# Batch 0's value block means as TensorE products with a banded matrix, instead of a second load and a tree of adds

## The chip, the cores and the metric

One core of one Trainium2 chip runs the whole program as a single launch. The metric is device time in microseconds (us). Engines: PE is TensorE (PEld its weight loads), DVE is VectorE, ACT is ScalarE, POOL is GpSimd, SP is SyncE, which here issues every DMA.

## What is computed

Block-sparse attention followed by two feed-forward networks, all in float32. Cut to what matters here:

```python
batch, n_heads, seq, head_dim = 2, 8, 768, 64
block, window, nb = 32, 16, 24                    # nb = seq // block
k_sum = k.reshape(B, H, nb, block, D).max(axis=3)
v_sum = v.reshape(B, H, nb, block, D).mean(axis=3)     # the value block means
scores_l = scale * q @ k.T        # kept only where |i - j| < window
scores_s = scale * q @ k_sum.T + log(block)
a = softmax(concat([masked scores_l, scores_s]))
attn = a @ concat([v, v_sum])
x = attn as (1536 tokens, 512)
x = prelu(x @ w_in, alpha) @ w_out              # 512 -> 2048 -> 512
out = silu(x @ w2_in) @ w2_out                  # 512 -> 2048 -> 512
```

## The kernel before

Heads are handled in pairs: 128 partitions hold 2 heads of 64 dimensions. There are 2 batches, 4 pairs, and blocks of 256 queries, so an attention step is (block, pair), and `order` lists 24 of them: batch 0's first two blocks pair by pair, then the rest block by block. A step n runs through `scores` (PE makes `sc` in a PSUM tile that has one buffer, DVE scales and masks it into `t` and takes its maximum `nm`), `exps` (ACT, `e` and the sums `sm`), `normalize` (DVE's reciprocal `rs`, then POOL multiplies `e`), `turn` (PE transposes `e` into `pt`, ACT copies it to `pT`) and `values` (PE multiplies `pT` with the value tile `vs` into `o`, ACT and DVE split that into `xh` and `xl` for the networks). Below, sc(n), t(n) and so on are those of step n.

A value tile `vs` has 120 rows for each of 12 sub-blocks of 64 queries: 96 rows are the window's raw values, 24 rows are the block means of the whole sequence. In an even sub-block the means are rows 0 to 23 and the window rows 24 to 119, in an odd one the window is rows 0 to 95 and the means are rows 96 to 119. The window rows come by two DMAs per pair (`vs<-in_vw`). For the means, `load_v` loads the same values a second time, transposed (`in_vT`, 384 KB per pair); `prep_v1` adds them down with two POOL adds (L482, 128x384 and 128x192) and one DVE reduction (`vr`, L485); `prep_v2` transposes `vr` on PE (L491) into the PSUM tile `pv`, and four ACT instructions (L495) scale it by 1/32 and copy it into the 12 places of `vs`. For batch 0 the transposed values lie in the half of the later output buffer `y` that `y_v` names; for batch 1 they go through the pool `stage`, whose 2 buffers they share with raw weights.

The weights come as raw 512 KB pieces (`load_next`, L116). A raw piece W(n) is converted (`conv_next`) by three DVE instructions (L142, L146, L149), one ACT cast (`wh`) and one POOL subtraction (`wl`). The first three raw pieces lie in the other half of `y` (`y_w`), the others in `stage`; a `stage` buffer is free again when DVE has read it.

The order of the first 100 us is a list of operations with hand-set due times (`AT_KEYS` and so on); a scheduling pass then orders each engine's instructions. Engines run their own list in order. SP issues the DMAs in one list, so a DMA that must wait for a buffer holds those behind it. `first_in` (L281 to L283, `ps<-xh,wl` and so on) is the first network product; the rest of the program after the attention is feed-forward products on PE.

Of the kernel before, what the change touches and what calls it, by code (L numbers as in the profile page):

```python
# [18 lines left out]
SUB = 64  # L19
PAD = WINDOW  # L20
WIN = SUB + 2 * PAD
P = 128
# [15 lines left out]
def tile_blocks_attention_mlps(  # L38
# [9 lines left out]
    consts: bass.AP,  # L48
    out: bass.AP,
# [34 lines left out]
    y_v = y.rearrange("p a n -> p (a n)")[:, :NPAIR * S].rearrange("p (a n) -> p a n", n=S)  # L84
    y_w = y.rearrange("p a n -> p (a n)")[:, NPAIR * S:].rearrange("p (a n w) -> p a n w", n=512, w=2)
# [341 lines left out]
    with ExitStack() as scope0:  # L427
# [4 lines left out]
        ps_s = scope0.enter_context(tc.tile_pool(name="ps_s", bufs=1, space=bass.MemoryType.PSUM))  # L432
        cst = kv.tile([P, P + 4 * NC], F32, name="cst", bufs=1)
        ident = cst[:, 0:P]
        mask = cst[:, P:]

# [8 lines left out]
        def load_v(b, p):  # L445
            if b == 0:
                t = y_v[:, p]
            else:
                t = stage.tile([P, 512, 2], F32, name="raw").rearrange("p n w -> p (n w)")[:, :S]
            nc.sync.dma_start(out=t, in_=vT[b, p])  # L450
            vt_t[b, p] = t
            t = kv.tile([NC, NSUB, P], F32, tag="vs", name="vs")
            vs_t[b, p] = t
            nc.sync.dma_start(out=t[NB:, 0::2], in_=vw[b, p, 0])
            nc.sync.dma_start(out=t[:WIN, 1::2], in_=vw[b, p, 1])
# [32 lines left out]
        def prep_v2(b, p):  # L488
            s_ = vs_t[b, p]
            pt = ps_mm.tile([P, 512], F32, tag="mm", name="pv")  # L490
            nc.tensor.transpose(pt[:NB, :P], vr_t.pop((b, p)), ident)  # L491

            def spread(s0, s1):
                for at in (s_[:NB, 2 * s0:2 * s1:2], s_[WIN:, 2 * s0 + 1:2 * s1:2]):
                    nc.scalar.activation(  # L495
                        out=at,
                        in_=pt[:NB, 0:P].unsqueeze(1).to_broadcast([NB, s1 - s0, P]),
                        func=AF.Copy,
                        scale=1.0 / BLOCK,
                    )  # L500
# [169 lines left out]
        for k, (blk, p) in enumerate(order[:2 * NPAIR]):  # L670
# [4 lines left out]
            if k == 0:  # L675
                at(first, lambda: nc.sync.dma_start(out=cst, in_=consts))
            if blk == 0:
                at(first, load_v, 0, p)
# [16 lines left out]
        def block_sums(b, p):  # L695
            prep_v1(b, p)
            if b:
                staged[0] -= 1
                flush()
# [102 lines left out]
def _layout(q, k, v, moe_w_in, moe_w_out, moe_alpha, moe2_w_in, moe2_w_out):  # L802
# [31 lines left out]
    for t, first in enumerate((0, P, S - P)):  # L834
# [5 lines left out]
        m[t, SUB:, :WIN] = np.where(ok, 0.0, -1000000000.0)[SUB:]  # L840
    consts = np.concatenate(
# [11 lines left out]
        "consts": np.ascontiguousarray(consts),  # L853
    }
# [19 lines left out]
```

## Time and profile before

| | us |
|---|---|
| median of 3 runs | 608.69 (608.2 to 609.58) |
| span of the profiled execution, first to last instruction | 604.6 |
| median less span: what lies around the instructions | 4.1 |
| PE busy | 576.8 (95% of the span) |
| DVE busy | 424.0 (70%) |
| ACT busy | 277.5 (46%) |
| POOL busy | 72.3 (12%) |

For the profiled execution the profile gives the span and no time of its own beside it, so the 4.1 us are taken from the median of the runs. A share of busy time is a mean over the span: the first 70 us (loads, attention, weight conversion) look quite different from the rest, in which PE runs products almost without a gap. A row of the timeline has the start, the duration, the engine, the line, output and inputs, the shape, the number of instructions merged into it, and in brackets how long the engine sat idle before and what ended that.

### The profile page before, as it was taken

The numbers are of one execution on the slowest core, as the hardware profiler recorded it, in microseconds if no ns is written. First come the engines' busy times: TensorE is split into PE (matmuls) and PEld (weight loads), VectorE is DVE, ScalarE is ACT, GpSimd is POOL, SyncE is SP. The second block draws the span as 40 slices with busy tenths as digits, with TensorE's granted clock in tenths as the row PEclk, the third lists the DMA queues.
The fourth block names the chain that finished last, engine by engine and source line by source line (L and its number), as shares of the span: only waits on it lengthen the run. The fifth ranks groups of instructions, "written<-read, shape, count | busy, mean of one in ns | idle before, by whom it ended". The sixth has DMA issues, their size and how long they took to land.

```text
span 604.6 us, 8927 instructions
## 1 busy us (share of the span) xinstructions
PE 576.8 (95%) x3428; PEld 483.5 (80%) x3428; DVE 424.0 (70%) x747; ACT 277.5 (46%) x636; POOL 72.3 (12%) x69
## 2 busy tenths in 40 slices
PE   2777999999999999999999999999999999999997
PEld 1556788999888888888888888888888888888886
DVE  3899979548995484349696879885972499965312
ACT  2768977654543341424544645543621245333200
POOL 2657654232100000000000000000000000000000
PEclk9988999999999999999999999999999999999999
DMA  9958754002351040003022002333130032200112
GB/s 263 341 193 260 231 147 140 2 2 70 140 154 56 0 140 0 1 1 112 28 69 70 1 1 79 131 117 93 32 108 0 1 111 96 73 1 0 54 69 88
DMA packets 31771, 52.54 MB, mean 87 GB/s; under 512 B 2288, under 2 KB 20976, under 8 KB 31728
## 3 DMA queue, kind: packets, MB, share of 16 engines
q1 hardware_dynamic: 31728, 51.97, 27.2%
q8 instruction: 27, 0.44, 0.3%
q14 instruction: 16, 0.13, 0.1%
HBM read 48.82 MB, written 3.15 MB: 86 GB/s over the span
## 4 chain that ended last, share of the span: by engine, by line
PE 82%; DVE 9%; DMA 3%; ACT 2%; SPq 1%; issue 1%; POOL 0%; DVEq 0%; POOLq 0%
PE ps L281 27%; PE ps L282 27%; PE ps L283 27%; DVE w L146 2%; DMA y<-in_w 1%; DVE w L149 1%; DMA vs<-in_vw 1%; DVE w L142 1%; DVE t L531 1%; DVE sm L557 1%; DVE nm L540 1%; PE o L579 1%; DVE kT L465 1%; ACT e L548 1%; DMA raw<-in_w 1%
## 5 line engine op out<-in xcount | busy, mean ns | idle before, releaser
L281 PE MATMUL ps<-xh,wl 128*128 128x512 f32 (+1 forms) x352 | 127.5, 367 | 1.2 <-ACT xh L587 1.2
L282 PE MATMUL ps<-xl,wh 128*128 128x512 f32 (+1 forms) x352 | 127.9, 364 | 0.0
L283 PE MATMUL ps<-xh,wh 128*128 128x512 f32 (+1 forms) x352 | 127.4, 363 | 0.0
L282 PE MATMUL ps<-gl,wh 128*128 128x512 f32 (+1 forms) x240 | 83.3, 348 | 0.0
L283 PE MATMUL ps<-gh,wh 128*128 128x512 f32 (+1 forms) x240 | 82.9, 346 | 0.0
L281 PE MATMUL ps<-gh,wl 128*128 128x512 f32 (+1 forms) x240 | 82.5, 350 | 0.0
L336 ACT CAST gh<-g 128x512 fp32r<-128x512 f32 x96 | 59.3, 622 | 46.2 <-PE ps L283 24.2
L281 PEld LDWEIGHTS ps<-xh,wl 128*128 128x128 f32 x352 | 66.5, 191 | 12.4 <-POOL e L560 1.4
L282 PEld LDWEIGHTS ps<-xl,wh 128*128 128x128 f32 x352 | 67.3, 191 | 10.2 <-issue 0.2
L283 PE MATMUL ps<-wh,gh 128*128 128x512 f32 (+1 forms) x196 | 75.4, 385 | 0.0
L283 PEld LDWEIGHTS ps<-xh,wh 128*128 128x128 f32 x352 | 67.3, 191 | 10.1
L282 PE MATMUL ps<-wl,gh 128*128 128x512 f32 (+1 forms) x196 | 75.4, 385 | 0.0
L281 PE MATMUL ps<-wh,gl 128*128 128x512 f32 (+1 forms) x196 | 75.2, 385 | 0.1
L337 DVE TENSOR_TENSOR gl<-g,gh 128x512 fp32r<-128x512 f32 x84 | 57.5, 687 | 20.7 <-ACT gh L336 20.3
L394 DVE TENSOR_TENSOR y<-ps,y 128x512 f32<-128x512 f32 x48 | 32.8, 689 | 45.4 <-PE ps L283 45.2
L324 ACT ACTIVATE g<-ps 128x512 f32<-128x512 f32 (+1 forms) x50 | 29.0, 579 | 70.8 <-PE ps L283 69.9
L155 ACT CAST wh<-w 128x512 fp32r<-128x512 f32 x64 | 39.3, 622 | 48.0 <-DVE w L149 43.5
L328 DVE SCALAR_TENSOR_TENSOR g<-m,nal,g 128x512 f32<-128x512 f32 (+1 forms) x60 | 41.4, 705 | 25.0 <-ACT m L325 24.9
L281 PEld LDWEIGHTS ps<-gh,wl 128*128 128x128 f32 x240 | 45.2, 189 | 6.6 <-issue 0.5
L282 PEld LDWEIGHTS ps<-gl,wh 128*128 128x128 f32 x240 | 45.4, 189 | 6.1 <-POOL gl L337 0.2
L283 PEld LDWEIGHTS ps<-gh,wh 128*128 128x128 f32 x240 | 45.3, 189 | 5.6
L146 DVE SCALAR_TENSOR_TENSOR w<-raw,w 128x512 uint32<-128x512 uint32 x61 | 44.6, 741 | 0.3
(82 smaller groups left out, 867.1 us busy)
## 6 DMA issues: line engine op xcount, KB each, us to landing
raw<-in_w SPq DMA_DIRECT2D x61, 512.0 KB, 3.8
vs<-in_vw SPq DMA_DIRECT2D x16, 288.0 KB, 5.6
kT<-in_kT SPq DMA_DIRECT2D x8, 480.0 KB, 5.2
q<-in_qT SPq DMA_DIRECT2D x24, 128.0 KB, 4.1
out<-y SPq DMA_DIRECT2D x11, 256.0 KB, 2.0
y<-in_vT SPq DMA_DIRECT2D x4, 384.0 KB, 6.5
y<-in_w SPq DMA_DIRECT2D x3, 512.0 KB, 7.7
raw<-in_vT SPq DMA_DIRECT2D x4, 384.0 KB, 4.5
```

The costliest lines, as they stand in the source:

```text
L142: nc.vector.tensor_scalar(out=w, in0=high, scalar1=3, scalar2=0x3FFFFFFF, op0=ALU.logical_shift_left, op1=ALU.bitwise_and,)
L146: nc.vector.scalar_tensor_tensor(out=w, in0=high, scalar=0xC0000000, in1=w, op0=ALU.bitwise_and, op1=ALU.bitwise_or)
L149: nc.vector.scalar_tensor_tensor(out=w, in0=low, scalar=29, in1=w, op0=ALU.logical_shift_right, op1=ALU.bitwise_or)
L155: nc.scalar.copy(out=hi, in_=w)
L281: nc.tensor.matmul(ps, all_, bh, start=first, stop=False)
L282: nc.tensor.matmul(ps, ah, bl, start=False, stop=False)
L283: nc.tensor.matmul(ps, ah, bh, start=False, stop=last)
L324: nc.scalar.activation(out=g[:, j * w:(j + 1) * w], in_=ps, func=AF.Relu)
L328: nc.vector.scalar_tensor_tensor(out=g[:, at], in0=m[:, at], scalar=nal[:, f + j:f + j + 1], in1=g[:, at], op0=ALU.mult, op1=ALU.add,)
L336: nc.scalar.copy(out=gh, in_=g)
L337: (nc.gpsimd if early else nc.vector).tensor_tensor(out=gl, in0=g, in1=gh, op=ALU.subtract)
L394: nc.vector.tensor_tensor(out=at, in0=src, in1=at, op=ALU.add)
```

## The change

Four edits, all about batch 0's value means:

- `load_v` no longer loads `in_vT` for batch 0, and `block_sums` runs `prep_v1` for batch 1 alone. Batch 1 stays as it was.
- A small constant `band` (128 x 2 x 44, 1/32 on the block each row belongs to, 0 elsewhere) is loaded once, after `cst`. `prep_v2` of batch 0 forms the 24 means in PSUM as the sum of 12 products, one per sub-block: the sub-block's 96 or 120 rows of `vs`, times the slice of `band` that picks its blocks. The copies out of PSUM scale by 1.
- Even sub-blocks are multiplied with all 120 rows, so the 24 mean rows must hold finite numbers first: POOL sets them to 0 (4 MEMSETs).
- `y_v` is gone and `y_w` covers all of `y`: six raw pieces lie in `y` instead of three.

```diff
-    y_v = y.rearrange("p a n -> p (a n)")[:, :NPAIR * S].rearrange("p (a n) -> p a n", n=S)
-    y_w = y.rearrange("p a n -> p (a n)")[:, NPAIR * S:].rearrange("p (a n w) -> p a n w", n=512, w=2)
+    y_w = y.rearrange("p a n -> p (a n)").rearrange("p (a n w) -> p a n w", n=512, w=2)
...
+        NBAND = 2 * NB - 4
+        band = kv.tile([P, 2, NBAND], F32, name="band", bufs=1)
...
         def load_v(b, p):
-            if b == 0:
-                t = y_v[:, p]
-            else:
+            if b:
                 t = stage.tile([P, 512, 2], F32, name="raw").rearrange("p n w -> p (n w)")[:, :S]
-            nc.sync.dma_start(out=t, in_=vT[b, p])
-            vt_t[b, p] = t
+                nc.sync.dma_start(out=t, in_=vT[b, p])
+                vt_t[b, p] = t
...
+            if b == 0:
+                nc.gpsimd.memset(t[:NB, 0::2], 0.0)
...
-            nc.tensor.transpose(pt[:NB, :P], vr_t.pop((b, p)), ident)
+            if b:
+                nc.tensor.transpose(pt[:NB, :P], vr_t.pop((b, p)), ident)
+            else:
+                for n in range(NSUB):
+                    rows, at = (WIN if n % 2 else NC), NB - 4 - 4 * (n // 2)
+                    nc.tensor.matmul(
+                        pt[:NB, :P], band[:rows, n % 2, at:at + NB], s_[:rows, n],
+                        start=n == 0, stop=n == NSUB - 1,
+                    )
...
-                        scale=1.0 / BLOCK,
+                        scale=1.0 / BLOCK if b else 1.0,
...
+                at(first, lambda: nc.sync.dma_start(out=band, in_=bands))
...
         def block_sums(b, p):
-            prep_v1(b, p)
             if b:
+                prep_v1(b, p)
                 staged[0] -= 1
                 flush()
```

The scheduling pass gives each engine a new order. Three places matter.

SP, the queue of loads, after the first key, query and `cst` loads (`kT` and `q` are keys and queries, `y<-in_w` and `raw<-in_w` raw weights). Before:

```order
L450 DMA y<-in_vT 128x768
L454 DMA vs<-in_vw 96x6x128
L455 DMA vs<-in_vw 96x6x128
L460 DMA q<-in_qT 128x256
L442 DMA kT<-in_kT 128x6x160
L460 DMA q<-in_qT 128x256
L450 DMA y<-in_vT 128x768
L454 DMA vs<-in_vw 96x6x128
L455 DMA vs<-in_vw 96x6x128
L460 DMA q<-in_qT 128x256
L116 DMA y<-in_w 128x1024
L442 DMA kT<-in_kT 128x6x160
```

and now:

```order
L687 DMA band<-in_bands 128x88
L456 DMA vs<-in_vw 96x6x128
L457 DMA vs<-in_vw 96x6x128
L462 DMA q<-in_qT 128x256
L444 DMA kT<-in_kT 128x6x160
L462 DMA q<-in_qT 128x256
L456 DMA vs<-in_vw 96x6x128
L457 DMA vs<-in_vw 96x6x128
L462 DMA q<-in_qT 128x256
L116 DMA y<-in_w 128x1024
L444 DMA kT<-in_kT 128x6x160
```

The four loads `y<-in_vT` are gone (two of them stand in this piece), `band` is new, and the first raw weights and the next keys move up.

PE, behind the first scores (before from pt(0) on, now from `pv` on; `sc` scores, `pt` transposes of `e`, `pv` value means, `o` values). Before:

```order
L566 MATMUL pt<-cst,e 120x128 x4
L491 MATMUL pv<-cst,vr 24x128
L523 MATMUL sc<-kT,q 64x120 x8
L566 MATMUL pt<-cst,e 120x128 x4
L579 MATMUL o<-pT,vs 64x64 x8
L523 MATMUL sc<-kT,q 64x120 x8
L566 MATMUL pt<-cst,e 120x128 x4
L579 MATMUL o<-pT,vs 64x64 x8
L491 MATMUL pv<-cst,vr 24x128
L523 MATMUL sc<-kT,q 64x120 x8
L566 MATMUL pt<-cst,e 120x128 x4
L579 MATMUL o<-pT,vs 64x64 x2
```

and now:

```order
L498 MATMUL pv<-vs,band 24x128 x12
L533 MATMUL sc<-kT,q 64x120 x8
L576 MATMUL pt<-cst,e 120x128 x4
L589 MATMUL o<-pT,vs 64x64 x2
L576 MATMUL pt<-cst,e 120x128 x4
L589 MATMUL o<-pT,vs 64x64 x6
L533 MATMUL sc<-kT,q 64x120 x8
L589 MATMUL o<-pT,vs 64x64 x8
L498 MATMUL pv<-vs,band 24x128 x12
L533 MATMUL sc<-kT,q 64x120 x8
L576 MATMUL pt<-cst,e 120x128 x4
L589 MATMUL o<-pT,vs 64x64 x2
```

Where one small transpose made `pv`, 12 products stand, ahead of sc(3) and again ahead of sc(5); the transposes of steps 1 and 2 have moved together.

DVE, from t(2) on before and from pair 2's keys on now, to t(3) (`kT` key maxima, `w` a raw weight piece being converted). Before:

```order
L531 SCALAR_TENSOR_TENSOR t<-sc,cst 128x480
L485 TENSOR_REDUCE vr<-y 128x24
L557 TENSOR_SCALAR sm<-sm 128x4
L540 TENSOR_REDUCE nm<-t 128x4
L142 TENSOR_SCALAR w<-y 128x512
L559 RECIPROCAL rs<-sm 128x4
L146 SCALAR_TENSOR_TENSOR w<-y,w 128x512
L465 TENSOR_REDUCE kT<-kT 128x24
L149 SCALAR_TENSOR_TENSOR w<-y,w 128x512
L531 SCALAR_TENSOR_TENSOR t<-sc,cst 128x480
```

and now:

```order
L569 RECIPROCAL rs<-sm 128x4
L473 COPY kT<-kT 128x6x24
L567 TENSOR_SCALAR sm<-sm 128x4
L569 RECIPROCAL rs<-sm 128x4
L142 TENSOR_SCALAR w<-y 128x512
L146 SCALAR_TENSOR_TENSOR w<-y,w 128x512
L149 SCALAR_TENSOR_TENSOR w<-y,w 128x512
L142 TENSOR_SCALAR w<-y 128x512
L541 SCALAR_TENSOR_TENSOR t<-sc,cst 128x480
```

In the old list t(3) stands right behind the first raw piece's three instructions, in the new one behind those of the second and the first of the third; the reductions `vr` are gone.

## Rows read from the trace of the kernel before

**Rows 1.** The page: the span, and PE's busy tenths in 40 slices of 15.1 us.
```profile
span 604.6 us, 8927 instructions
...
PE   2777999999999999999999999999999999999997
```

**Rows 2.** Busy time by stretch: PE, PEld, DVE, ACT, POOL, granted clock, DMA share, GB/s.
```profile
10.00:20.00 10.00, 5.45 (x57) 3.81 (x57) 6.75 (x17) 4.75 (x17) 3.83 (x4) 1.00 1.12 334
20.00:30.00 10.00, 8.31 (x83) 6.19 (x82) 9.45 (x18) 7.88 (x31) 6.86 (x7) 1.00 1.11 338
30.00:40.00 10.00, 7.70 (x68) 6.44 (x68) 9.93 (x20) 5.35 (x17) 6.78 (x7) 0.83 0.63 207
40.00:50.00 10.00, 7.33 (x114) 5.52 (x117) 9.96 (x20) 9.76 (x37) 5.89 (x6) 1.00 0.67 216
50.00:60.00 10.00, 6.82 (x98) 5.49 (x91) 10.00 (x22) 7.41 (x28) 7.75 (x8) 0.83 0.88 253
60.00:70.00 10.00, 8.97 (x138) 7.56 (x136) 9.66 (x23) 8.81 (x36) 4.87 (x6) 1.00 0.69 220
```

**Rows 3.** DMA issues to 70 us: count, KB of each, median us to landing.
```profile
vs<-in_vw SPq DMA_DIRECT2D x14, 288.0 KB, 6.0
kT<-in_kT SPq DMA_DIRECT2D x8, 480.0 KB, 5.2
...
q<-in_qT SPq DMA_DIRECT2D x21, 128.0 KB, 4.0
y<-in_vT SPq DMA_DIRECT2D x4, 384.0 KB, 6.5
y<-in_w SPq DMA_DIRECT2D x3, 512.0 KB, 7.7
```

**Rows 4.** Timeline of POOL: the adds for pairs 1, 2 and 3.
```profile
13.70 1.00 POOL L482 TENSOR_TENSOR y<-y 128x384 f32<-128x384 f32 x1 [3.91 <-DMA y<-in_vT]
...
20.33 1.69 POOL L482 TENSOR_TENSOR y<-y 128x384 f32<-128x384 f32 x2 [1.22 <-DMA y<-in_vT]
...
29.59 2.00 POOL L482 TENSOR_TENSOR y<-y 128x384 f32<-128x384 f32 x2 [0.90 <-DMA y<-in_vT]
```

**Rows 5.** Timeline of DVE, 13 to 34 us.
```profile
13.22 0.22 DVE L471 COPY kT<-kT 128x144 f32<-128x144 f32 x1
...
17.12 0.42 DVE L142 TENSOR_SCALAR w<-y 128x512 uint32<-128x512 uint32 x1
...
17.58 0.69 DVE L146 SCALAR_TENSOR_TENSOR w<-y,w 128x512 uint32<-128x512 uint32 x1
18.49 0.95 DVE L465 TENSOR_REDUCE kT<-kT 128x24 f32<-128x768 f32 x1 [0.22 <-DMA kT<-in_kT]
19.36 0.68 DVE L149 SCALAR_TENSOR_TENSOR w<-y,w 128x512 uint32<-128x512 uint32 x1
...
23.29 1.19 DVE L142 TENSOR_SCALAR w<-y 128x512 uint32<-128x512 uint32 x1 [0.55 <-DMA y<-in_w]
...
27.48 0.64 DVE L540 TENSOR_REDUCE nm<-t 128x4 f32<-128x480 f32 x1
...
31.07 0.62 DVE L471 COPY kT<-kT 128x144 f32<-128x144 f32 x1
...
33.09 0.34 DVE L485 TENSOR_REDUCE vr<-y 128x24 f32<-128x192 f32 x1
```

**Rows 6.** Timeline of PE: pt(0), sc(5), and a later pt.
```profile
15.70 1.11 PE L566 MATMUL pt<-cst,e 128*120 128x128 f32 x4 [1.14 <-POOL e L560]
...
26.66 1.08 PE L523 MATMUL sc<-kT,q 64*64 64x120 f32 x16
...
36.70 1.05 PE L566 MATMUL pt<-cst,e 128*120 128x128 f32 x4
```

**Rows 7.** The chain that ended last: four transposes on PE.
```profile
109.56 0.44 PE pt L566 x4
```

**Rows 8.** Busy time by stretch, columns as in the second group.
```profile
36.60:40.00 3.40, 3.40 (x29) 2.94 (x28) 3.40 (x8) 1.59 (x3) 2.76 (x2) 0.50 0.65 200
```

More of the change, by code (lines that the diff above doesn't have):

```diff
@@ L48, in tile_blocks_attention_mlps @@
     consts: bass.AP,
+    bands: bass.AP,
     out: bass.AP,
@@ L840, in _layout @@
         m[t, SUB:, :WIN] = np.where(ok, 0.0, -1000000000.0)[SUB:]
+    bands = np.zeros((P, 2, 2 * nb - 4), np.float32)
+    for odd, row in ((0, nb + pad), (1, pad)):
+        for i in range(SUB // BLOCK):
+            at = nb - 4 + 2 * odd + i
+            bands[row + i * BLOCK:row + (i + 1) * BLOCK, odd, at] = 1.0 / BLOCK
     consts = np.concatenate(
@@ L853, in _layout @@
         "consts": np.ascontiguousarray(consts),
+        "bands": bands,
     }
```

## The prediction

> **What bounds the kernel now.** I begin with the page. PE's line [rows 1] is full from the sixth slice to the last but one, so nothing that happens after some 75 us can be gained except by taking work off PE; the change takes none off there. What it can move is the beginning. The stretches of 10 us [rows 2] show it: DMA is the full resource to 30 us (share over 1, 334 to 338 GB/s), DVE is busy 9.45 to 10.00 of 10 us from 20 to 70 us, and PE has room. The room between pt(0) at 15.7 us [rows 6] and 70 us is the sum of PE's gaps: 1.69 + 2.30 + 2.67 + 3.18 + 1.03 from the rows of 20 to 70 us, and about 1.1 in 15.7 to 20 us (busy 5.45 in that row, of which two scores, run before pt(0), have 2 x 1.08 [rows 6]): 12.0 us. So the first stage waits for loads, then for DVE, then the program is PE's, and the end follows from when PE becomes full and from how much work it then has left.
>
> **Loads.** DMA runs at a steady pace. POOL's adds for pairs 1 and 2 start when `y<-in_vT` lands, at 13.70 and 20.33 us [rows 4]; between these two, in SP's order, lie two `vs`, two `q`, one weight, one `kT` and the second `in_vT`: 2 x 288 + 2 x 128 + 512 + 480 + 384 = 2208 KB [rows 3] in 6.63 us, 0.0030 us per KB. Each `in_vT` taken away is 384 KB, 1.15 us; `band` adds 44 KB once. Pair 1's keys move up by 340 KB, 1.0 us. The first weight W(0), two `in_vT` fewer ahead, moves by 724 KB, 2.2 us; from 13.70 plus 1216 KB, 17.35, to 15.2 us. Pair 2's keys come at 16.3 instead of 18.49 us [rows 5]. W(1), three fewer, moves by 1108 KB, 3.3 us: DVE waited for it till 23.29 [rows 5], now 19.9 us. W(2) follows 640 KB later, 21.9 us, pair 3's keys at 23.3 us. W(3) to W(5) no longer wait for a `stage` buffer, but DVE, not their arrival, sets when they are converted; I give that nothing.
>
> **POOL and DVE.** Eight adds go. In the rows shown they take 1.7 to 2.0 us per pair [rows 4]. DVE loses four reductions of 0.34 us [rows 5]; three stood before the point I compare at, below. A copy of 0.22 us took 0.62 at 31.07, inside the add of 29.59 [rows 4, 5]: 0.4 us of DVE that I count as gained. The four MEMSETs are new on POOL, each over 768 columns. No row shows that form; an add over 384 and 192 columns takes 1.69 to 2.0 us, so I bound one by 0 and 2 us. They run from 0.4 us, and the first thing POOL is now asked for is step 0's normalization at about 13.4 us: hidden even at 8 us in all.
>
> **PE's new work.** A plain float32 product is two recorded passes (eight products of sc are x16 in [rows 6]), so 12 products are 24 passes of 128 columns. The nearest row is the transpose, one pass of 128 columns: four take 0.44 us at the high level (2.4 GHz) [rows 7], 0.11 each. At the low level they take 1.05 (granted clock 0.50 there [rows 6, 8]); pt(0) at 15.70 takes 1.11, so PE is at the low level (1.2 GHz) there too, although the clock column shows 1.00 for that stretch: it has no record so early. A run of 24 passes is then 2.6 us high, 5.3 us low. The bounds are wider: 1.08/16 = 0.07 us a pass, as in sc, where four quarter-array products run side by side, and 1.11/4 = 0.28 us, the transposes with their tail; 1.6 to 6.7 us at the low clock. I take 5.3 and 2.6. The four transposes that go take about 0.25 us each, 1.0 us together.
>
> **Walking the first 35 us.** DVE: pair 1's keys at 10.7, t(1), step 0's reciprocal at 13.3; POOL normalizes to 14.4, and pt(0) starts at 14.4 instead of 15.70. The first run of products is 15.4 to 20.7 us at the low clock, its `vs` landed long before. sc(3) and its t(3) come late, but DVE's new order has W(0), W(1) and the first of W(2) ahead of t(3) anyway: at 22.3 us it asks for t(3), and sc(3) is done at 21.8. DVE then finishes nm(4) at about 28.1 us, as it did before (27.48 + 0.64 [rows 5]), but with more behind it: two more instructions of W(2) (0.69 + 0.68), the first of W(3) (0.42), pair 3's keys (0.95 + 0.22), less one reciprocal of 0.17: **2.8 us ahead**; the fourth reduction, 0.34, and the slowed copy, 0.4, make it 3.5 us.
>
> The second run stands ahead of sc(5), and t(5) waits for sc(5). DVE reaches t(5) at 30.0 us. Behind sc(3), at 21.8 us, PE has pt(1), o(0) in two pieces, pt(2), sc(4) and o(1) before the second run: five groups of about 1.0 us at the low clock, so the run starts at 26.9 us: run 5.3, sc(5) 1.08 [rows 6], ready at 33.3, and DVE loses 3.3 us. If the clock has risen, PE is waiting for DVE by then and sc(5) is ready at about 30.2: 0.2 us lost. Runs three and four stand, in PE's order, before the places where the old trace has PE idle (2.67 and 3.18 us in the rows from 40 and from 50 us [rows 2]), and what is queued behind them, the scores of steps 8 and 11, is asked for by DVE several instructions later; at 2.6 us each they are covered. That cover is gone if PE is already behind.
>
> So the clock decides between 15 and 30 us. In the old trace it was low through transposes, scores and values from 15.7 to 28.7 us, and it rose at 40.0 [rows 8] in a stretch that ended in network products without transposes between them. A run of 24 plain passes without a pause resembles the second more than the first; I take it that the clock is up before the second run. The Trainium skill, TensorE: Matmul & The Clock Gate (Part 4: PE-mode transpose), says that transposes do not count as PE being busy for the clock. The trace agrees as far as the stretch to 28.7 us, with transposes in it, stayed low; by that rule the exchange of a transpose for products would itself help to raise it, and the sum is the forecast's, without it rival A's.
>
> **The sum.** DVE's lead is 3.5 - 0.2 = 3.3 us. PE has to follow: it gets 5.3 + 3 x 2.6 - 1.0 = 12.1 us more, and about 5 us less, since some 11 us of work between 20 and 33 us runs at the high level instead of the low; 7 us net against a room of 12.0 + 1.3 (earlier start). If the end moved by the full 3.3 us, PE would have only 3 us of gaps left in 52, where it had 12; I give a third back for that: **-2.2 us**. Span 604.6 - 2.2 = 602.4; with the 4.1 us around it, which lie between the span and the median, **606.5 us**. Its own range, from no third lost and 1.2 us more of relieved DVE to two thirds lost: 605.0 to 608.0.
>
> **Rivals.**
> *A: the clock stays low through the second run, and the gain is eaten there.* DVE loses 3.3 of its 3.5 us at t(5), and PE works off its backlog in the old gaps. For it: the old trace has no products of this shape, so no row shows the clock rise behind them, and it was low over all that PE did before 28.7 us. 608.7 us, 607.3 to 610.5.
> *B: PE becomes the bound of the first stage.* With three runs low and one high, 3 x 5.3 + 2.6 - 1.0 = 17.5 us are added against 13.3 us of room: +4.2 us, 612.9, and 610 to 615 with the unknown length of a pass. It decides from 13.3 us of added work on. For it: PE executes in order, and a late `pv` holds scores that do not need it. Against it: the two late runs lie where the old trace ran at the high clock.
> *C: POOL's adds cost DVE all their time.* If each of the 3.7 us of adds after 20 us [rows 4] stopped DVE, the relief is 3.7 instead of 0.4 us; with a third given back, about 604.3 us. Against it: DVE was busy through that stretch, not stopped (9.45 and 9.93 of 10 us [rows 2]), and the copy is the one instruction that I could tie to an add behind 28 us. The Trainium skill, SBUF — State Buffer (SBUF: two separate sides), has DVE and POOL share a port pair that is locked for a whole instruction, for some DVE forms; the copy of 0.62 us agrees with it, the whole 3.7 us do not.
> *D: the loads do not land earlier*, because SP issues and the queue's depth, not bytes, set the pace. Then only PE's extra work is left: about 609.5. Against it: 334 GB/s over the whole stretch.
>
> **Chances.** Forecast 0.45, A 0.22, B 0.20, C 0.08, D 0.05. About 0.2% (1.2 us) is what a measurement can tell from no change: faster is below 607.5, slower above 609.9. Faster: 0.39 of the forecast, 0.08 of C, 0.01 of A, together 0.48. Same: 0.06, 0.14 of A, 0.04 of D: 0.24. Slower: 0.20 of B, 0.07 of A, 0.01 of D: 0.28. The range from 604.5 to 611.8 leaves out half of C and most of B, and some of each tail.
>
> **What the changed profile should show.** DVE's first instruction of W(1) at about 20 us (D says 23); pt(0) at about 14.4; the first run of `pv` 5.3 us long; the second, at 26 to 28 us, 2.6 us long with PE waiting soon after (A and B: 5.3 us, and DVE waiting for sc(5) some 3 us). PE's busy time should rise by about 7 us (B: by 13 or more) and its gaps to 70 us shrink from 12 to about 4. I am wrong if a run takes more than 6.7 us, or if DVE in 35 to 65 us is no longer full because it waits for PE.

## The result, and the profile after

The changed kernel takes **615.29 us** (median of 4 runs, 613.36 to 617.41) against 608.52 (4 runs, 608.2 to 609.58): a ratio of 1.0098, 95% interval 1.0069 to 1.0127. It is slower by 1.0%, some 6 to 7 us, outside the range and on the other side of the forecast. Each of these runs is some 1.8 us longer than its span (615.28 us for the profiled 613.5). If that holds for the kernel before too, the 604.6 us of the old profile [rows 1] belong to an execution of 606.4, some 2 us under the median of its runs. So the 4.1 us of the table above the prediction are not all time around the instructions, and the spans lie 2 us further apart than the medians.

The page of the changed kernel: its span, the engines' busy time, and PE's tenths in 40 slices.

```profile
span 613.5 us, 9099 instructions
...
PE 584.8 (95%) x3520; PEld 490.9 (80%) x3520; DVE 422.5 (69%) x743; ACT 278.1 (45%) x636; POOL 67.3 (11%) x65
...
PE   2888897999999999999999999999999999999997
```

PE's busy time rises by 8.0 us from the 576.8 in the table above the prediction; I had said about 7. What I had not said is where it shows. The same columns as in [rows 2], for the changed kernel:

```profile
10.00:20.00 10.00, 6.79 (x58) 5.00 (x59) 6.36 (x15) 3.88 (x19) 0.99 (x1) 1.00 1.15 281
20.00:30.00 10.00, 6.94 (x86) 5.07 (x84) 8.98 (x13) 5.07 (x15) 4.65 (x4) 0.80 1.10 318
30.00:40.00 10.00, 8.61 (x73) 6.82 (x75) 9.96 (x19) 8.60 (x32) 6.21 (x5) 0.69 0.61 229
40.00:50.00 10.00, 7.87 (x108) 6.33 (x100) 10.00 (x19) 6.33 (x23) 5.47 (x5) 1.00 0.25 79
50.00:60.00 10.00, 8.75 (x123) 7.08 (x123) 9.39 (x22) 7.76 (x27) 8.46 (x9) 1.00 0.91 269
60.00:70.00 10.00, 8.08 (x129) 6.55 (x129) 8.88 (x20) 9.20 (x36) 5.99 (x7) 1.00 0.61 180
...
90.00:100.00 10.00, 6.64 (x85) 5.44 (x83) 7.34 (x15) 9.74 (x31) 3.67 (x3) 1.00 0.48 159
```

From 20 to 70 us PE is idle for 9.75 us, where it was 10.87 [rows 2], and from 15.7 to 20 us it is now full. So its gaps to 70 us went from 12.0 to 9.75 us; they were to shrink to about 4. A new gap of 3.4 us stands at 90 to 100 us, where PE used to be full. One row puts it together, the first 110 us of each kernel (columns as before). Before:

```profile
0.00:110.00 110.00, 85.43 (x968) 71.20 (x972) 90.72 (x180) 78.42 (x264) 59.83 (x59) 0.97 0.73 217
```

The changed kernel:

```profile
0.00:110.00 110.00, 84.68 (x971) 70.53 (x974) 86.63 (x169) 73.81 (x248) 51.42 (x52) 0.94 0.70 197
```

PE has been busy for 85 us by then in both, though the changed kernel has 8 us more to do. What is left behind 110 us is 576.8 - 85.4 = 491.4 us before and 584.8 - 84.7 = 500.1 now, and PE works it off almost without a gap: 8.7 of the 8.9 us between the spans. Over the whole span PE is idle for 27.8 us before (604.6 - 576.8) and for 28.7 now (613.5 - 584.8). So the new work took no gap; other work was pushed out of the first 110 us, and that work is paid at the end.

What was pushed out is the attention. PE's waits from 10 to 110 us, the view of waits of the changed kernel:

```profile
PE sc L533 <- DVE t L541: 11.2, 7, 2.4
PE sc L533 <- DMA q<-in_qT: 2.8, 1, 2.8
PE pt L576 <- POOL e L570: 2.7, 3, 1.4
```

Before, scores waited for `t` 3.9 us in 3 waits. The runs of products, and scores and pieces that wait, in the timeline of PE of the changed kernel:

```profile
16.28 4.16 PE L498 MATMUL pv<-vs,band 120*24 120x128 f32 x24
...
20.37 0.64 PE L533 MATMUL sc<-kT,q 64*64 64x120 f32 x16
...
26.14 1.08 PE L533 MATMUL sc<-kT,q 64*64 64x120 f32 x16 [2.43 <-DVE t L541]
...
28.20 5.00 PE L498 MATMUL pv<-vs,band 120*24 120x128 f32 x24
...
43.15 2.82 PE L498 MATMUL pv<-vs,band 120*24 120x128 f32 x24
...
54.95 2.82 PE L498 MATMUL pv<-vs,band 120*24 120x128 f32 x24
...
99.42 0.64 PE L533 MATMUL sc<-kT,q 64*64 64x120 f32 x16 [2.28 <-DVE t L541]
```

And DVE around t(3), the timeline of the changed kernel:

```profile
16.17 0.43 DVE L142 TENSOR_SCALAR w<-y 128x512 uint32<-128x512 uint32 x1 [2.12 <-DMA y<-in_w]
...
22.13 0.65 DVE L142 TENSOR_SCALAR w<-y 128x512 uint32<-128x512 uint32 x1 [0.76 <-DMA y<-in_w]
22.82 1.64 DVE L146 SCALAR_TENSOR_TENSOR w<-y,w 128x512 uint32<-128x512 uint32 x1
24.49 0.69 DVE L149 SCALAR_TENSOR_TENSOR w<-y,w 128x512 uint32<-128x512 uint32 x1
25.10 0.42 DVE L142 TENSOR_SCALAR w<-y 128x512 uint32<-128x512 uint32 x1
25.44 0.65 DVE L541 SCALAR_TENSOR_TENSOR t<-sc,cst 128x480 f32<-128x480 f32 x1
...
28.52 0.64 DVE L550 TENSOR_REDUCE nm<-t 128x4 f32<-128x480 f32 x1
```

In the timeline of the kernel before, t(3) was:

```profile
19.95 0.65 DVE L531 SCALAR_TENSOR_TENSOR t<-sc,cst 128x480 f32<-128x480 f32 x1
```

sc(3) is ready at 21.0 us, but DVE's list has W(1) and the first of W(2) ahead of t(3), and W(1) lands only at 22.1. nm(3) comes at 28.5, and sc(4), which needs the one buffer of `sc`, waits for t(3) till 26.1. nm(4) is done at 31.8 us; the prediction had 28.1. t(3) and t(4) are 5 us late; later steps are 1 to 5 us late up to t(17).

The loads, by the view of DMA from 0 to 27 us. Before:

```profile
DMA packets 9066, 8.16 MB, mean 302 GB/s; under 512 B 382, under 2 KB 8049, under 8 KB 9065
```

Changed:

```profile
DMA packets 9446, 7.19 MB, mean 266 GB/s; under 512 B 493, under 2 KB 8896, under 8 KB 9445
```

The queue moves fewer bytes in the same time and about as many pieces. The transposed loads that went were rows of 3 KB; the window values (`vs`) that stay come in pieces of 512 bytes.

### The profile page after: what moved, and what is told of

Read it like the earlier page. It is cut to its first block, busy times and chain, and to the rows that moved or that the text cites. A ratio compares the mean times of both kernels' runs of the same rounds, so it can differ in the third digit from the quotient of the medians.

```text
span 613.5 us, 9099 instructions
## 1 busy us (share of the span) xinstructions
PE 584.8 (95%) x3520; PEld 490.9 (80%) x3520; DVE 422.5 (69%) x743; ACT 278.1 (45%) x636; POOL 67.3 (11%) x65
## 4 chain that ended last, share of the span: by engine, by line
PE 85%; DVE 6%; DMA 4%; SPq 2%; issue 1%; ACT 1%; POOL 0%; DVEq 0%
PE ps L281 27%; PE ps L282 27%; PE ps L283 27%; DMA raw<-in_w 2%; DVE w L146 2%; DMA y<-in_w 1%; PE o L589 1%; DVE w L142 1%; PE pt L576 1%; DMA kT<-in_kT 1%; SPq L462 1%; DVE t L541 1%; PE sc L533 1%; DVE w L149 1%; SPq L457 1%
## 5 line engine op out<-in xcount | busy, mean ns | idle before, releaser
L328 DVE SCALAR_TENSOR_TENSOR g<-m,nal,g 128x512 f32<-128x512 f32 (+1 forms) x60 | 39.4, 672 | 27.9 <-ACT m L325 27.8
L558 ACT ACTIVATE e<-t,nm 128x120 f32<-128x120 f32 x96 | 36.8, 388 | 16.9 <-DVE nm L550 16.8
```

Source lines behind the costliest of these rows:

```text
L328: nc.vector.scalar_tensor_tensor(out=g[:, at], in0=m[:, at], scalar=nal[:, f + j:f + j + 1], in1=g[:, at], op0=ALU.mult, op1=ALU.add,)
L558: nc.scalar.activation(out=e[:, u, :], in_=t[:, u, :], func=AF.Exp, bias=nm[:, u:u + 1], accum_out=sm[:, u:u + 1],)
```

## The experiments

Ratios are to runs of the kernel before on the same chip, with 95% intervals. The groups of runs were on different chips; across groups the ratios are compared.

### One part at a time, in whatever order the scheduling pass makes

**One product of twelve.**

```diff
-                for n in range(NSUB):
+                for n in range(1):
...
-                        start=n == 0, stop=n == NSUB - 1,
+                        start=True, stop=True,
```

> The changed kernel with one of the twelve products of each run (its value means are those of the first sub-block alone; eleven products are left out), loads and everything else as changed. Theory P (the time is the products' own PE time, 14.8 us of runs in the changed kernel, because PE's old gaps can't take it): about 13.5 us of PE work go, and the time falls below the kernel before, to 600 to 605 us. Theory O (the time is the new order: the raw weights of the second stage come late because batch 1's transposed values hold the two staging buffers): the gap of 3.4 us in 90 to 100 us stays, and the time is 608 to 612 us.

Measured: 615.38 us, ratio 1.0104 (1.0068 to 1.0139). The same as the change, although some 13 us of runs are gone. Theory P in its plain form falls, and the 608 to 612 us of theory O are missed as well.

**The kernel before, with the products added** (band, MEMSETs and the 12 products ahead of the transpose that overwrites them):

```diff
+            if not b:
+                for n in range(NSUB):
+                    rows, at = (WIN if n % 2 else NC), NB - 4 - 4 * (n // 2)
+                    nc.tensor.matmul(
+                        pt[:NB, :P], band[:rows, n % 2, at:at + NB], s_[:rows, n],
+                        start=n == 0, stop=n == NSUB - 1,
+                    )
             nc.tensor.transpose(pt[:NB, :P], vr_t.pop((b, p)), ident)
```

> The kernel before with all its loads, adds and reductions, plus the change's runs of products ahead of its transposes, their result overwritten by the transpose. Theory P: 9 to 13 us slower than before, 617 to 622 us, more than the change itself, since no load is saved. Theory O: the products find room, 609 to 612 us.

Measured: 624.28 us, 1.0258 (1.0220 to 1.0296), more than either theory allowed. The two runs contradict each other as long as one thinks that only the products differ: the pass had ordered all engines anew in both.

**Three raw weights in `y` as before.**

```diff
-    y_w = y.rearrange("p a n -> p (a n)").rearrange("p (a n w) -> p a n w", n=512, w=2)
+    y_w = y.rearrange("p a n -> p (a n)")[:, NPAIR * S:].rearrange("p (a n w) -> p a n w", n=512, w=2)
```

> The changed kernel with three raw weights in y as before, the other half of y unused. Theory P and the prediction's step on W(3) to W(5), which gave their earlier arrival nothing: the same as the change, 613.5 to 616.5 us. Theory O, in the form that six early weights push their conversion ahead of the attention's steps on DVE: 609 to 612 us.

Measured: 616.84 us, 1.0121 (1.0081 to 1.0160); it cannot be told from the change. W(3) to W(5) in `y` give nothing, as the prediction had it.

**Batch 1's transposed values in buffers of their own**, so that raw weights do not wait for `stage` behind them; these values are then asked for at once, outside the queue that `stage` needs.

```diff
-                t = stage.tile([P, 512, 2], F32, name="raw").rearrange("p n w -> p (n w)")[:, :S]
+                t = kv.tile([P, S], F32, tag="vt", name="vt", bufs=2)
```

> The changed kernel with batch 1's transposed values in two buffers of their own instead of the staging buffers, so that they never hold up a raw weight. Theory O: the gap at 90 to 100 us (3.4 us) and the low clock behind it (about 1.7 us) go, 609.5 to 611.5 us. Theory P: the time is PE's work, PE's busy time stays near 585 us, and the time stays within 1.5 us of the change, 613.8 to 616.8 us.

Measured: 619.24 us, 1.0160 (1.0132 to 1.0187), where theory O asked for 609.5 to 611.5. The gap at 90 to 100 us did go (PE 10.00 of 10 us), but 4.7 us of gaps stand at 70 to 90 us instead. The pass had ordered the engines anew here too, so this speaks against theory O without settling it.

### The order held fixed

From here on an engine's list can be fixed: `LISTS` holds, per engine, the places of the instructions in the wanted order, and each is tied behind the one before it. These ties only fix the order.

```diff
+LISTS = {
...
+        traced = list(nc.cur_bb.bb.instructions)
+        for places in LISTS.values():
+            for a, b in zip(places, places[1:]):
+                tc.add_manual_dep(
+                    traced[b], traced[a].name,
+                    mybir.DependencyInfo(mybir.DependencyClass.NoSync, mybir.DependencyReason.DATA),
+                    reason="list",
+                )
```

**The change in the order of before** (lists of all five engines).

> The changed kernel, with every engine's list held to the order of the kernel before (edges that fix the order and wait for nothing): the 12 products stand where the one transpose stood, the band load behind cst, the four MEMSETs first on POOL; nothing is left out. Theory S (the loss is the new order that the scheduling pass made, weights ahead of scores on DVE): 606 to 609.5 us, PE's waits for DVE's t back to some 4 us. Theory C (the loss is the change's own work, the products and the loads, whatever the order): 613 to 617 us.

**The same with one product of twelve.**

> As the run in the old order, with only the first of the 12 products of each pair (the other 11, so the means of 11 of 12 sub-blocks, are left out). This prices the products in a fixed order. If they lie in PE's gaps, as the prediction had it, 605.5 to 608.5 us and within 1 us of the run with all 12; if they are paid in full, 8 to 13 us below that run.

**The change with DVE's list alone in the order of before.**

> The changed kernel with DVE's list alone in the order of the kernel before; the pass orders the other engines around it. Theory S, with DVE's list as its cause: 606 to 611 us. If PE's or SP's order is what costs, or theory C holds: 613 to 617 us.

**The kernel before in the order of the change** (PE, DVE, ACT).

> The kernel before, with the lists of PE, DVE and ACT in the order of the changed kernel (the reductions of batch 0's sums stand behind the same neighbour as before; one transpose where the 12 products stand). Theory S: 613 to 618 us although no product is added. Theory C: 607 to 610 us.

**The change in its own order, with one product of twelve.**

> The changed kernel in its own order, held fixed, with only the first of the 12 products of each pair (the other 11 are left out). With the run in the old order this makes a square: two orders, with and without the products. If the products cost the same in both orders (5.4 us in the old one), 609 to 611 us. If the new order alone makes the loss, 613 to 616 us. If the products alone do, 607 to 609 us.

Measured:

| | 12 products | 1 product |
|---|---|---|
| order of before | 1.0088 (1.0053 to 1.0123), 613.46 us | 0.9992 (0.9967 to 1.0017), 608.01 us |
| order of the change | 1.0098 (1.0069 to 1.0127), 615.29 us | 1.0115 (1.0078 to 1.0152), 617.62 us |

DVE's list alone: 611.24 us, 1.0048 (1.0019 to 1.0077). The kernel before in the new order: 618.81 us, 1.0149 (1.0113 to 1.0185).

So neither is the cause by itself. In the old order the products cost 5.4 us (613.46 - 608.01) and without them the change is no different from before: theory S does not hold there, theory C does. In the new order the same loss is there with or without products: there S holds. The column without products also tells what the rest of the change (loads, POOL, DVE) is worth in the old order: -0.1%, nothing, where I had 3.5 us of lead. (The profiled execution of the run with one product, at 613.05 us the longest of its ten, shows a lower clock than the run with 12 products, 0.86 against 0.95 over the first 110 us; what the clock took there is not separated.)

What the new order does without any products is seen in the kernel before in that order: PE's waits from 10 to 110 us, and t(3) in DVE's timeline.

```profile
PE sc L523 <- DVE t L531: 13.8, 9, 3.1
```

```profile
29.82 0.65 DVE L531 SCALAR_TENSOR_TENSOR t<-sc,cst 128x480 f32<-128x480 f32 x1
```

There t(3) stands behind W(1), which DVE takes up at 26.26 us, and the first of W(2), as in the changed kernel. It comes 10 us later than in the old order (19.95), and scores wait 13.8 us for `t` where they waited 3.9. This run still has the transposed loads, so W(1) lands some 4 us later in it than in the changed kernel.

How the products cost 5.4 us in the old order is read from ACT. The copies of the means into `vs`, the timeline of ACT in the run in the old order with 12 products:

```profile
19.45 1.98 ACT L505 ACTIVATE vs<-pv 24x256 f32<-24x256 f32 x4 [2.82 <-PE pv L498]
...
32.32 1.38 ACT L505 ACTIVATE vs<-pv 24x256 f32<-24x256 f32 x3 [3.49 <-PE pv L498]
```

They stand ahead of the exponentials of the next step, so ACT waits for the run of products, then the exponentials, the reciprocal on DVE and the multiplication on POOL come late, and PE pays with its next transposes:

```profile
26.11 1.11 PE L576 MATMUL pt<-cst,e 128*120 128x128 f32 x4 [4.42 <-POOL e L570]
```

That is pt(2). In the kernel before, the one transpose (0.42 us in PE's timeline) held nobody. The Trainium skill, PSUM — Partial Sum Buffer (Engine vs sequencer instructions), says that the queues of ScalarE, VectorE and GpSimd are strictly first in, first out, and that matmuls start and complete in program order; the waits of 2.82, 3.49 and 4.42 us agree.

In the run with one product the same two copies wait for nothing, and pt(2) waits for 1.16 us:

```profile
17.47 1.98 ACT L505 ACTIVATE vs<-pv 24x256 f32<-24x256 f32 x4
...
28.54 1.38 ACT L505 ACTIVATE vs<-pv 24x256 f32<-24x256 f32 x3
```

```profile
25.28 1.11 PE L576 MATMUL pt<-cst,e 128*120 128x128 f32 x4 [1.16 <-POOL e L570]
```

PE's gaps stay open with the 12 products in the list, 11.4 us from 20 to 70 us (columns as before):

```profile
20.00:70.00 50.00, 38.55 (x474) 30.44 (x474) 42.89 (x85) 36.94 (x134) 25.46 (x22) 0.90 0.67 202
```

### The pace of the loads

**The value tile with even and odd sub-blocks apart**, so that a row of a value load is one piece of 3072 bytes instead of six of 512; the same edit in the kernel before and in the change, both in the order of before, and in the change in its own order.

```diff
-            t = kv.tile([NC, NSUB, P], F32, tag="vs", name="vs")
+            t = kv.tile([NC, 2, NTWO, P], F32, tag="vs", name="vs")
...
-            nc.sync.dma_start(out=t[NB:, 0::2], in_=vw[b, p, 0])
-            nc.sync.dma_start(out=t[:WIN, 1::2], in_=vw[b, p, 1])
+            nc.sync.dma_start(out=t[NB:, 0], in_=vw[b, p, 0])
+            nc.sync.dma_start(out=t[:WIN, 1], in_=vw[b, p, 1])
```

> The kernel before in its own order, held fixed, with one thing changed: the value tile keeps even and odd sub-blocks apart, so that a row of a value load is one piece of 3072 bytes instead of six of 512 (96 pieces a load instead of 576). Theory N (the pace of the loads is set by the number of pieces, not by bytes): the first raw weights land 3 us or more earlier, 603 to 607 us. Theory K (bytes, 0.0030 us per KB, as the prediction had it): nothing lands more than 0.5 us earlier, 607.5 to 609.5 us.

> The changed kernel in the old order, with the value tile laid out in rows of 3072 bytes as in the run before this. Theory N: the loads are ahead by as much as in that run, and the time is below the run in the old order (613.5 us) by 2 us or more, 607 to 611 us, still above the kernel before with the same layout by the price of the products, 3 to 6 us. Theory K: 612.5 to 614.5 us.

> The changed kernel in its own order, with the value tile in rows of 3072 bytes (96 pieces a load instead of 576). In the old order this brought the second raw weight's issue from 14.4 to 13.1 us and the last keys' from 17.8 to 14.3. Theory W: DVE no longer stands at the second raw weight (22.1 us) and the time falls by 3 us or more, 609 to 612 us. If not: 614 to 616.5 us.

Measured: the kernel before with these rows 608.08 us against 609.73, 0.9957 (0.9938 to 0.9976); the change in the old order 612.75, 1.0048 (1.0026 to 1.0069), after 1.0088 without the rows; the change in its own order 613.44, 1.0058 (1.0039 to 1.0077), after 1.0098. Each time some 0.4%; the first difference is clear of noise by itself, in the other two the intervals overlap. The view of DMA from 0 to 27 us: the kernel before with these rows, the change in the old order without and with them, and the change in its own order with them:

```profile
DMA packets 5883, 8.20 MB, mean 304 GB/s; under 512 B 386, under 2 KB 4213, under 8 KB 5882
```

```profile
DMA packets 9214, 6.96 MB, mean 258 GB/s; under 512 B 483, under 2 KB 8696, under 8 KB 9213
```

```profile
DMA packets 6057, 8.12 MB, mean 301 GB/s; under 512 B 656, under 2 KB 4528, under 8 KB 6056
```

```profile
DMA packets 5840, 7.61 MB, mean 282 GB/s; under 512 B 587, under 2 KB 4427, under 8 KB 5839
```

Neither theory holds by itself. With fewer pieces and all the bytes, the rate stays at 304 GB/s, W(2) is issued at 16.76 instead of 17.74 us, and theory N's 3 us do not come. With fewer bytes and all the pieces (the change) the rate falls to 266, in the old order to 258. Only with both do the loads come earlier by what I had worked out: in the old order, at 301 GB/s over a third fewer pieces, W(2) is issued at 13.09 instead of 17.31 us, the last keys at 14.26 instead of 17.79. In the change's own order the rate rises less, to 282 GB/s, and W(2) is issued at 13.99 instead of 16.66 us. (The expectation of the last run calls 13.1 us the second raw weight's issue; it is the third's, the second's is 11.76.) Theory W's 3 us do not come in that last run either: W(1) starts at 20.79 instead of 22.13 us on DVE, t(3) at 24.40 instead of 25.44.

### Where the products stand

**Four groups of columns and a fold.**

```diff
-                        pt[:NB, :P], band[:rows, n % 2, at:at + NB], s_[:rows, n],
-                        start=n == 0, stop=n == NSUB - 1,
+                        pt[32 * j:32 * j + 32, P:2 * P], band[:rows, n % 2, at:at + 32], s_[:rows, n],
+                        start=n < 4, stop=n >= NSUB - 4,
                     )
+                part = kv.tile([P, P], F32, tag="part", name="part", bufs=1)
+                nc.scalar.copy(out=part, in_=pt[:, P:2 * P])
+                nc.tensor.matmul(pt[:NB, :P], fold, part, start=True, stop=True)
```

> The changed kernel in the old order, with the 12 products in four groups of columns that lie side by side on PE, a copy of the four partial sums by ACT, and one product that folds them; nothing is left out. If what the products cost is the time that PE is held by them in front of the scores (5.4 us of the run in the old order for 14 us of runs), a run falls from 2.8 to 5.3 us to 1.5 to 2.5 us and the time to 608.5 to 611.5 us. If it is their number or the clock behind them, 612.5 to 614.5 us.

Measured: 611.91 us, 1.0030 (1.0005 to 1.0054), 0.6% below the run in the old order. A run and its fold take 1.3 to 2.1 us of PE instead of 2.8 to 4.1. This fits the reading that the products cost what they hold up.

**Each run behind the next scores, the copies behind the next exponentials.** In the lists (first run):

```diff
 PE  pt(0)
-PE  pv x12
 PE  sc(3)
+PE  pv x12
...
 ACT pT(0)
-ACT vs x4
 ACT e(2)
+ACT vs x4
```

> The changed kernel in the old order, but each run of 12 products stands behind the next scores on PE instead of ahead of them, and on ACT the copies of the means stand behind the next four exponentials instead of ahead of them. Nothing else moves and no work is taken away. Theory Q (the products cost what they hold up in the queues of PE and ACT): 3 us or more below the run in the old order (613.5), 608 to 610.5 us, and ACT's waits for pv fall from 3 us to below 1. Theory T (their PE time itself costs): 612.5 to 614.5 us.

Measured: 614.23 us, 1.0065 (1.0041 to 1.0089). Not what theory Q asked for: ACT still waits 2.33, 2.39 and 1.86 us for `pv`, and values now wait for the copies (2.32 and 1.46 us). The wait only moved, and the time cannot be told from the run in the old order.

**t and nm of steps 3 to 8 ahead of the weights, in the change's own order.**

```diff
+DVE t(3), nm(3)
 DVE W(1) x2
+DVE t(4), nm(4)
 DVE W(1), W(2)
-DVE t(3)
...
```

> The changed kernel in its own order, with one thing moved in DVE's list: t and nm of steps 3 to 8 stand where as many weight instructions are ahead of them as in the kernel before (3, 5, 9, 14, 18, 20 instead of 7, 9, 12, 17, 19, 24). Theory W (t behind weights that have not landed is what the new order costs): 609 to 612 us. If the new order loses elsewhere: 614 to 617 us.

Measured: 624.91 us, 1.0245 (1.0218 to 1.0272), 9 us worse. Theory W falls in this form. DVE now stands at t(5), the timeline of DVE and of PE in this run:

```profile
34.61 0.66 DVE L541 SCALAR_TENSOR_TENSOR t<-sc,cst 128x480 f32<-128x480 f32 x1 [4.87 <-PE sc L533]
```

```profile
28.76 5.22 PE L498 MATMUL pv<-vs,band 120*24 120x128 f32 x24
```

The second run of products stands ahead of sc(5). That is the stall of rival A (3.3 us there, 4.87 here). As long as PE's list has the runs ahead of the scores, the weights ahead of `t` are what DVE does meanwhile, and moving `t` alone only trades one wait for another. It does not show that the weights cost nothing: without products, above, the scores wait for the `t` behind them.

**Each run ahead of a place where PE waited** in the run in the old order; in PE's list, no work taken away. (The call that makes the means moves ahead in the program for this; the other engines' lists keep their order.)

```diff
 PE  sc(1)
+PE  pv x12
 PE  sc(2), pt(0)
-PE  pv x12
 PE  sc(3), pt(1), o(0), sc(4)
+PE  pv x12
 PE  pt(2), o(1)
-PE  pv x12
 PE  sc(5)
...
```

> The changed kernel in the old order, but each run of 12 products stands ahead of a place where PE waited in the run in the old order: the first ahead of sc(2) (a wait of 2.15 us), the second ahead of pt(2) (4.42), the third ahead of pt(4) (1.80 and 0.41 near it), the fourth ahead of pt(6) (0.84). No work is taken away. Theory Q (the products cost what they hold up; in a wait with landed operands they cost less): at least 6 of the 14 us of runs fall into waits, PE's busy time in the first 110 us rises from 86 to 89 us or more, 608.5 to 611 us. Theory T (the waits are those of a chain that the runs lengthen wherever they stand): 612.5 to 615 us, PE's busy time to 110 us stays at 85 to 87.

**The same with the rows of 3072 bytes.**

> As the run before this, with the value tile in rows of 3072 bytes, which gave 0.4% in three other pairs of runs. Theory Q: 606 to 609 us. Theory T: 610 to 613 us.

Measured: 610.62 us, 1.0034 (1.0005 to 1.0063), and with the rows 609.01 us, 1.0003 (0.9983 to 1.0022). Theory Q: the place alone is worth some 0.5% (1.0034 against 1.0088, and with the rows 1.0003 against 1.0048, where the intervals lie apart). Theory T falls. It is not that the runs became shorter: they take 15.7 us in all here and 13.2 in the old order. The runs in PE's timeline of the first of the two:

```profile
11.26 5.21 PE L498 MATMUL pv<-vs,band 120*24 120x128 f32 x24
...
22.30 2.82 PE L498 MATMUL pv<-vs,band 120*24 120x128 f32 x24
...
35.85 4.87 PE L498 MATMUL pv<-vs,band 120*24 120x128 f32 x24
...
47.17 2.82 PE L498 MATMUL pv<-vs,band 120*24 120x128 f32 x24
```

and the first two copies on ACT, which wait for nothing:

```profile
18.14 1.97 ACT L505 ACTIVATE vs<-pv 24x256 f32<-24x256 f32 x4
...
27.41 1.38 ACT L505 ACTIVATE vs<-pv 24x256 f32<-24x256 f32 x3
```

PE's busy time in the first 110 us, for the run in the old order and for this one, then with the rows, again in the old order and with the runs moved:

```profile
0.00:110.00 110.00, 85.99 (x996) 70.58 (x996) 84.67 (x167) 73.01 (x243) 52.77 (x52) 0.95 0.72 198
```

```profile
0.00:110.00 110.00, 87.55 (x1024) 72.09 (x1025) 84.62 (x171) 75.27 (x253) 54.69 (x53) 0.97 0.72 203
```

```profile
0.00:110.00 110.00, 88.77 (x983) 73.16 (x984) 84.97 (x165) 73.34 (x243) 53.05 (x52) 0.92 0.64 197
```

```profile
0.00:110.00 110.00, 89.95 (x1047) 74.48 (x1048) 86.48 (x174) 77.68 (x263) 55.78 (x55) 0.97 0.69 203
```

It rises from 86.0 to 87.6, less than the 89 that theory Q asked, and with the rows from 88.8 to 90.0. Busy time at a low clock is not the same work, so what is left behind 110 us tells more, PE's busy time in all less these: 584.0 - 86.0 = 498.0 us in the old order and 583.0 - 87.6 = 495.4 here, with the rows 587.6 - 88.8 = 498.8 and 582.6 - 90.0 = 492.6. Now some of the gaps are used. The mean granted clock is higher with the runs moved, too (0.97 against 0.95 and 0.92); no run separates what that gave.

**DVE's list of before, the rows and the column groups together.**

> The change with DVE's list as in the kernel before, the value tile in rows of 3072 bytes, and the products in four groups side by side with one folding product. If the three gains found singly (0.4, 0.4 and 0.6% of 608 us against the run in the old order at +0.9%) add up: 604.5 to 607 us, below the kernel before and level with the kernel before with the same rows. If they overlap: 607 to 610 us.

Measured: 614.19 us, 1.0068 (1.0040 to 1.0096). The single gains do not add up. Here the second run begins at 22.7 us and its fold stands 8 us behind its end; whether that is why is open.

The fastest version of all is the kernel before with the rows of 3072 bytes: 0.4% below the kernel before, 1.4% below the change.

## Why the prediction was wrong, step by step

**The step that failed** is the one that set PE's new 7 us "against a room of 12.0 + 1.3": PE's gaps as room. The 7 us were about right (8.0 came), but the gaps to 70 us went from 12.0 only to 9.75 where about 4 were forecast, and over the whole span none of them was used. They were the waits of a chain, PE to DVE to ACT to POOL and back to PE, with one buffer for `sc`. A run of products in front of sc, or in front of ACT's copies, makes the chain longer by its length, and the gap opens again behind it: in the old order PE was still idle 11.4 us from 20 to 70 us. The same runs, placed in waits with their operands landed, cost some 3 us less (1.0034 against 1.0088). The prediction had the right sentence, "PE executes in order, and a late `pv` holds scores that do not need it", and gave it to rival B as an argument; B's own mechanism, 13.3 us of work filling all gaps, did not happen (+8.0); that its 610 to 615 us end next to the measured time is luck. The queue behind ACT's copies I did not see at all.

A second step failed beside it, and in the change's own order the loss is there without the products. "sc(3) and its t(3) come late, but DVE's new order has W(0), W(1) and the first of W(2) ahead of t(3) anyway" was counted as DVE's lead, and what the late `t` costs PE was put at nothing. Scores waited for `t` for 11.2 us, where it had been 3.9; in the kernel before in the new order it was 13.8, and that kernel lost 1.5% with no product in it.

**Loads: mis-sized.** 0.0030 us per KB, 1.15 us for each transposed load. It was worked out over a mixture of long and short pieces; the loads that went were the long ones. Pair 1's keys came at 11.49 (forecast 10.7, before 11.71), W(0) at 16.17 (15.2), W(1) at 22.13 (19.9, before 23.29). Of leads of 1.0, 2.2 and 3.3 us came 0.2, 1.2 and 1.2 (W(0) against the prediction's own 17.35).

**DVE 3.5 us ahead: wrong.** It rested on these loads, and on DVE's instructions keeping their short times. t(3) did wait for nothing but DVE's own list, but it came at 25.44 us instead of 22.3, and nm(4) was done at 31.8 instead of 28.1: W(1) landed 2.2 us late, and the second instructions of W(1) and W(2), at 22.82 and 26.00 us, took 1.64 and 1.73 us instead of 0.69. POOL's subtractions for `wl` ran beside both (22.46 to 23.91 and 25.91 to 27.18 us); that they are the reason is not shown. Without the products the whole lead was worth nothing measurable in the old order (0.9992).

**The price of a run: right.** 5.3 us at the low clock and 2.6 at the high one was the forecast. 4.16, 5.00, 2.82 and 2.82 came, 14.8 us in all against 13.1, mostly because the second run was at the low clock. **The clock: half right.** It rose within the first run: sc(3) behind it takes 0.64 us, the time of the high level. It was low again after PE had waited 2.43 us for DVE (sc(4) at 26.14 takes 1.08; granted clock 0.80 and 0.69 in the rows of 20 and 30 us), so the second run was low most of the way, as in rival A. In the kernel before, too, the clock had risen before the 40.0 us of the prediction: the sc at 34.30 us takes 0.64 us there, behind network products, and the pt at 36.70 is low again.

**t(5) and A: right as a mechanism.** The stall was 4.87 us where DVE had nothing else ahead of it. In the changed kernel itself weights stand there, and the lateness goes to the attention instead.

**W(3) to W(5), the MEMSETs, POOL's adds: right.** Three in `y` or six makes no difference, the MEMSETs lie ahead of everything, and C's 3.7 us did not appear in the time: in the old order without products the rest of the change is worth nothing. **D** was right in part: something other than bytes sets the pace once the long pieces are gone.

**My own test** said: wrong "if DVE in 35 to 65 us is no longer full because it waits for PE". DVE stayed nearly full there (10.00 and 9.39 in the rows of 40 and 50 us; 28.62 of the 30 us, before 29.92). The test looked at busy time; DVE was busy with the weights that the new list had moved ahead. Two other signs missed: pt(0) came at 15.25 us instead of 14.4, and the second run was 5.0 us long instead of 2.6.

What is open: how much of the 1.15% that the change's own order loses without the products is the `t` behind the weights, and what the rest is; and why DVE's old list alone is better (1.0048) than all five old lists (1.0088), whose intervals overlap.

## What to carry to other kernels

An idle stretch of an engine is room for new work only if the new work's operands have landed when it begins and nothing that others wait for is queued behind it; look at what stands behind it on its own engine, and behind its reader on the reader's. Before pricing a load that goes by bytes, compare the length of its pieces with that of the loads that stay. And when an edit makes a scheduling pass order everything anew, hold one order fixed first: here one part taken out gave the same time, and the same part put in elsewhere +2.6%, until the lists were tied.

## What the runs showed of the hardware that I had not expected

A queue of loads that stayed busy throughout moved 7.19 MB in 27 us where it had moved 8.16 (266 against 302 GB/s), once four loads with rows of 3 KB were gone from it; W(2) was issued 1.1 us earlier (16.66 against 17.74). With a third of its pieces gone instead (9066 to 5883, 304 GB/s) it was 1.0 us; with both 4.7 us in the old order (13.09) and 3.8 in the change's own (13.99). The Trainium skill, DMA: Bandwidth & Descriptors (Specifications), gives 512 bytes as the least transfer for full rate; a queue made mostly of pieces of 512 to 640 bytes did not reach here what it reached with rows of 3 KB (258 against 301 GB/s in the old order, 266 against 282 in the change's own).

A run of 24 plain float32 passes with a 24-column stationary operand raised the granted clock from its low level (1.2 GHz) to its high one (2.4 GHz) within itself, where transposes, scores and values had left it low up to 28.7 us in the kernel before. It did not do so each time: the first run, moved ahead to 11.26 us, took 5.21 us, low to its end, and only the sc behind it was high (0.64 us). A pass took 2.82/24 = 0.12 us at the high level, close to what I had taken from the transposes (0.11).
